# Decode attention on one core: keys and values on two DMA queues with two fixed slots each

## The chip, the cores and the metric

The kernel runs on one core of a Trainium2 chip. The metric is the device time of one execution in microseconds (us). Executions of this kernel are repeatable: the kernel before took 1296.13 to 1296.38 us in four executions. The span of a profile is about 2 us shorter than the time of the same execution. The program uses one core, so there is no comparison of dies to be made.

Words used below: TensorE, VectorE, ScalarE and SyncE are engines of the core, each with its own list of instructions. An engine *issues* a transfer with one instruction; the transfer then stands in that engine's DMA queue (q1 is SyncE's here, q10 ScalarE's) and is carried by the sixteen DMA engines as *packets*, one record of the profile each. It has *landed* when its data can be used. A *slot* is a part of the on-chip buffer `ring` that holds one tile.

## The reference

One decode step of a block: layer norm, attention of one new token over a cache of 8192 positions, output projection, and a gated feed-forward part.

```python
B, Sq, D = 4, 1, 512
H, Sk, Dh = 32, 8192, 128
q = (layernorm(x) @ wq).reshape(B, Sq, H, Dh).transpose(0, 2, 1, 3)
scores = einsum("bhqd,bhkd->bhqk", q, k_cache) * Dh ** -0.5
o = einsum("bhqk,bhkd->bhqd", softmax(scores), v_cache)
h = x + o.transpose(0, 2, 1, 3).reshape(B, Sq, H * Dh) @ wo
hn = layernorm(h)
out = h + (sigmoid(hn @ w_gate) * (hn @ w_up)) @ w_down      # F = 1792
```

All inputs are bfloat16. Each cache has 4 x 32 x 8192 x 128 x 2 bytes = 268 MB, so the caches are 537 MB of the 551 MB that the kernel reads; every byte of them is used once.

## The kernel before

A *tile* is the keys, or the values, of two heads: 128 partitions of 32 KB, 4 MB. There are 64 key tiles and 64 value tiles. The kernel works head by head (`s` counts heads, `t` counts tiles): VectorE transposes the keys of a head into `kT` (four instructions), TensorE multiplies them with the queries (`pe_score`), and after each group of eight heads the exponential is taken. The value product of a head (`pe_pv`) is done ten heads after its scores (`LAG = 10`), so value tile `t` is needed only when key tile `t + 5` has been scored.

All tiles go through four slots of 32 KB per partition, in one order, on one queue: SyncE issues every transfer. A slot is given to the next item in the list, whatever it is.

```python
        items = [("wq", 0)]
        for t in range(NT2 + LAG2):                 # NT2 = 64 tiles, LAG2 = 5
            if t < NT2:
                items.append(("k", t))
            if t >= LAG2:
                items.append(("v", t - LAG2))
            for i in {LAG2 - 4: (0, 1), LAG2 - 3: (2, 3, 4), LAG2 - 2: (5, 6, 7)}.get(t - NT2, ()):
                items.append(("wo", i))             # output weights: eight pieces, among the last values
        items += [("wg", 0), ("wu", 0), ("wd", 0)]  # feed-forward weights: behind everything
        # ... cut: bookkeeping
        for it in items:
            # ... cut: wo goes to kT, wu shares wg's slot
            slot_of[it] = cur
            prev_of[it] = [owner[cur]] if owner[cur] is not None else []
            owner[cur] = it
            cur = (cur + 1) % NS                    # NS = 4
        # ... cut
        for it in items:
            dma_of[it] = [P("sp", fn, (), sem, val) for fn, sem, val in load(it)]
        # ... cut: at the end, an item waits until the slot's former owner is consumed
                op.deps = [sc_of[NST - 1]] if it[0] == "wo" else [consumed[p] for p in prev_of[it]]
```

In the middle of the run keys and values alternate in the list, so a stream already has two slots in effect. At the start the list holds keys 0 to 5 in a row, and they pass through all four slots. The rows of a tile are 32 KB in memory; those of wo and of the down weights are 1 KB, those of the gate and up weights 3584 B.

## Time and profile before

The median is 1296.3 us. What matters of its profile (span 1294.5 us):

| | |
|---|---|
| share of the sixteen DMA engines' time on queue q1 | 99.5% |
| rate in the middle of the span (130 to 1200 us) | 431 GB/s |
| VectorE, TensorE, ScalarE busy | 48%, 39%, 4% of the span |
| last piece of the last value tile is waited for until | 1277.45 us |
| last piece of the down weights is waited for until | 1291.18 us |

The page of the kernel before, the rates in 40 slices of the span, the DMA queues (packets, MB, share of the sixteen engines' time), the chain of work that ended last, and the issues of keys and values (number, size of each, median us from issue to landing):

```profile
GB/s 405 434 428 432 432 428 433 431 430 430 433 431 430 433 429 431 433 427 433 434 426 434 431 427 435 429 431 435 425 434 432 426 435 428 431 434 429 429 376 322
...
q1 hardware_dynamic: 26016, 550.78, 99.5%
...
DMA 81%; PE 12%; SPq 4%; DVE 3%; issue 0%
...
ring<-in_A_k_cache_dram SPq DMA_DIRECT2D x64, 4096.0 KB, 29.7
ring<-in_A_v_cache_dram SPq DMA_DIRECT2D x63, 4096.0 KB, 34.0
```

The engines move 425 to 435 GB/s in every slice but the first and the last two, and the chain that decides the end is 81% DMA. A tile of 4 MB takes 9.71 us at the median between one landing and the next (landing times in the trace), but 30 to 34 us from issue to landing: each waits behind two or three others. So the queue always has work.

The end of the kernel before, from the chain of work that ended last (start us, us, what):

```profile
1279.05 12.10 DMA ring<-in_B_w_down_dram
1291.14 0.04 issue
1291.19 0.60 PE PS L637 x16
...
1291.81 0.20 DVE oT L643
...
1292.37 0.28 DVE o_sb L648
```

The last thing waited for is the last piece of the down weights, and only 1.5 us of compute and the store of the result follow it. The last value piece came 13.7 us earlier (1291.18 - 1277.45); the rest of the attention, the layer norm and the gate and up products ran under the weights' transfer.

There was one short stretch of idle DMA engines in this tail. Value tile 62 takes the slot of value tile 58, which TensorE had finished with at 1221.3 us. But SyncE was in three issues of wo until 1244.6 us and issued the tile only then (start us, us, engine, line, operation), and between 1240 and 1248 us the DMA share was 0.86:

```profile
1221.95 22.66 SPq L220 DMA_DIRECT2D kT<-in_A_wo_dram  x3
1244.66 2.31 SPq L256 DMA_DIRECT2D ring<-in_A_v_cache_dram  x1
...
1240.00:1248.00 8.00, 1.91 (x12) 1.78 (x8) 0.17 (x1) 0.00 (x0) 0.00 (x0) 0.50 0.86 316
```

### The profile page before, as it was taken

Reading aid. Unit: us, or ns where it says so; the run is one execution under the profiler, and the core shown is the slowest. Engines: PE = TensorE matmul, PEld = TensorE weight load, DVE = VectorE, ACT = ScalarE, POOL = GpSimd, SP = SyncE. Lnnn points to the kernel's source line nnn. Section 1 sums busy time; section 2 is a strip of 40 time slices with the busy share of each in tenths; the row PEclk is TensorE's granted clock in tenths of the full one; section 3 lists DMA queues with packets and bytes.
Section 4 is the critical chain, followed back from the end, with each engine's and each line's share of the span. In section 5 each row is a group of like instructions: output and inputs, shape, how many; then the busy total and the mean of one; then the engine's idle time right before and its main releaser. Section 6 shows DMA issues by size and latency. Waiting matters only on the chain.

```text
span 1294.5 us, 12693 instructions
## 1 busy us (share of the span) xinstructions
PE 499.5 (39%) x5827; PEld 193.4 (15%) x5827; DVE 625.4 (48%) x641; ACT 46.1 (4%) x102; POOL 10.6 (1%) x22
## 2 busy tenths in 40 slices
PE   3444334335244244334334334343343343343436
PEld 1011111112011021111111111011110111111114
DVE  5964644535544544535535435445535446445300
ACT  2000000000000000000000000000000000000000
POOL 3000000000000000000000000000000000000000
PEclk9996565665565565565666665665665665656655
DMA  9999999999999999999999999999999999999998
GB/s 405 434 428 432 432 428 433 431 430 430 433 431 430 433 429 431 433 427 433 434 426 434 431 427 435 429 431 435 425 434 432 426 435 428 431 434 429 429 376 322
DMA packets 26076, 551.58 MB, mean 426 GB/s; under 512 B 2340, under 2 KB 8232, under 8 KB 9256
## 3 DMA queue, kind: packets, MB, share of 16 engines
q1 hardware_dynamic: 26016, 550.78, 99.5%
q8 instruction: 45, 0.74, 0.2%
q14 instruction: 7, 0.06, 0.0%
q10 hardware_dynamic: 8, 0.00, 0.0%
HBM read 550.77 MB, written 0.00 MB: 425 GB/s over the span
## 4 chain that ended last, share of the span: by engine, by line
DMA 81%; PE 12%; SPq 4%; DVE 3%; issue 0%
DMA ring<-in_A_v_cache_dram 79%; PE PS L439 7%; PE PS L415 4%; SPq L220 2%; DVE kT L397 2%; SPq L236 1%; DMA ring<-in_A_wq_dram 1%; DMA ring<-in_B_w_down_dram 1%; SPq L228 1%; SPq L256 0%; PE PS L330 0%; DVE Lq L374 0%; DVE ring L347 0%; PE PS L357 0%; PE PS L637 0%
## 5 line engine op out<-in xcount | busy, mean ns | idle before, releaser
L397 DVE STREAM_TRANSPOSE kT<-ring 128x1024 uint32<-128x1024 uint32 x512 | 587.9, 1209 | 578.8 <-DMA ring<-in_A_k_cache_dram 578.6
L415 PE MATMUL PS<-kT,Lq 128*32 128x512 bf16 x2048 | 241.6, 619 | 563.3 <-DVE kT L397 443.8
L439 PE MATMUL PS<-ring,PTz 128*32 128x512 bf16 x2048 | 215.0, 564 | 208.7 <-DMA ring<-in_A_v_cache_dram 208.3
L415 PEld LDWEIGHTS PS<-kT,Lq 128*32 128x32 bf16 x2048 | 69.4, 135 | 692.4 <-DVE kT L397 471.9
L439 PEld LDWEIGHTS PS<-ring,PTz 128*32 128x32 bf16 x2048 | 64.5, 127 | 326.4 <-DMA ring<-in_A_v_cache_dram 197.1
L474 ACT ACTIVATE negm<-PS 128x1 f32<-128x1 f32 x16 | 2.7, 171 | 1156.3 <-PE PS L470 1156.3
L511 DVE TENSOR_SCALAR Zs<-PS,rinv 128x512 f32<-128x512 f32 x16 | 11.6, 723 | 36.4 <-PE PS L439 36.4
L506 ACT ACTIVATE PTz<-PS 64x512 bf16<-64x512 f32 x32 | 18.9, 592 | 16.5 <-PE PS L492 16.1
L518 PE MATMUL PS<-SelZ,Zs 128*128 128x8 f32 x128 | 19.1, 276 | 0.9 <-DVE Zs L511 0.9
L518 PEld LDWEIGHTS PS<-SelZ,Zs 128*128 128x128 f32 x128 | 17.6, 213 | 10.6 <-issue 8.9
L453 DVE TENSOR_REDUCE mx<-PS 128x1 f32<-128x512 f32 x16 | 10.5, 658 | 5.4 <-PE PS L415 5.4
L492 PEld LDWEIGHTS PS<-Sel,E_sb 128*32 128x32 bf16 x1024 | 10.4, 96 | 8.3 <-ACT E_sb L476 7.1
L492 PE MATMUL PS<-Sel,E_sb 128*32 128x32 bf16 x1024 | 11.0, 183 | 1.6 <-ACT E_sb L476 1.1
L476 ACT ACTIVATE E_sb<-PS,negm 128x512 bf16<-128x512 f32 x16 | 11.0, 688 | 0.5
L481 PEld LDWEIGHTS PS<-sig,Gsum 128*128 128x128 f32 x32 | 7.8, 305 | 12.6 <-issue 12.6
L481 PE MATMUL PS<-sig,Gsum 128*128 128x1 f32 x32 | 9.2, 356 | 0.0
L470 PEld LDWEIGHTS PS<-onesf,rowx 1*128 1x128 f32 x32 | 7.3, 281 | 13.0 <-issue 13.0
L470 PE MATMUL PS<-onesf,rowx 1*128 1x1 f32 x32 | 8.6, 336 | 0.0
L523 DVE CAST OT<-PS 128x8 bf16<-128x8 f32 x16 | 2.1, 132 | 11.6 <-PE PS L518 11.6
L347 DVE CAST ring<-PS 128x512 bf16<-128x512 f32 x4 | 2.5, 683 | 10.0 <-PE PS L330 10.0
L485 DVE RECIPROCAL rinv<-PS 128x1 f32<-128x1 f32 x16 | 2.1, 130 | 9.3 <-PE PS L481 9.3
L330 PE MATMUL PS<-ring,xnT 128*32 128x512 bf16 x32 | 3.6, 629 | 6.6 <-DMA ring<-in_A_wq_dram 6.6
(78 smaller groups left out, 81.3 us busy)
## 6 DMA issues: line engine op xcount, KB each, us to landing
ring<-in_A_k_cache_dram SPq DMA_DIRECT2D x64, 4096.0 KB, 29.7
ring<-in_A_v_cache_dram SPq DMA_DIRECT2D x63, 4096.0 KB, 34.0
ring<-in_A_wq_dram SPq DMA_DIRECT2D x1, 4096.0 KB, 12.3
kT<-in_A_wo_dram SPq DMA_DIRECT2D x8, 512.0 KB, 17.3
ring<-in_A_v_cache_dram SPq DMA_DIRECT2D x1, 2048.0 KB, 18.5
ring<-in_A_v_cache_dram SPq DMA_DIRECT2D x2, 1024.0 KB, 18.2
ring<-in_B_w_gate_dram SPq DMA_DIRECT2D x1, 1792.0 KB, 19.9
ring<-in_B_w_up_dram SPq DMA_DIRECT2D x1, 1792.0 KB, 23.5
```

Source lines behind the costliest of these rows:

```text
L220: return [(lambda e: e.dma_start(wo_v[:, HW * t:HW * t + HW, :], A_wo.rearrange("(h p) f -> p h f", p=128)[:, HW * t:HW * t + HW, :]).then ...
L228: return e.dma_start(ringv(slot)[:, c0:c1], kv_src(t, A_v_cache)[:, c0:c1]).then_inc(s_piece[i], 16)
L236: return e.dma_start(wd_v[:, t0:t1, :], B_w_down.rearrange("(t p) f -> p t f", p=128)[:, t0:t1, :]).then_inc(s_piece[3 + i], 16)
L397: return e.transpose(kT[:, buf, i * q:(i + 1) * q].bitcast(U32), ringv(src)[:, base + i * q:base + (i + 1) * q].bitcast(U32))
L415: mm = e.matmul(bS[g % 2][32 * j:32 * (j + 1), :], Lq[:, l0:l0 + 32], rhs, start=(s % GS == 0 and v == 0), stop=(s % GS == GS - 1 and v == 3),
L439: mm = e.matmul(bO[g % 2][32 * rq:32 * (rq + 1), :], PTz[:, g % 2, l0:l0 + 32], ringv(slot)[:, r0 * 128:(r0 + 4) * 128], start=(s % GS == ...
L470: p2_of[g] = P("pe", lambda e: e.matmul(bX[:, 0:1], rowx[0:1, :], onesf[0:1, 0:1], start=True, stop=True), [d2b_of[g], c_ones])
L481: L_of[g] = P("pe", lambda e: e.matmul(bX[:, 0:1], Gsum[:, :], sig[:, 0:1], start=True, stop=True), [exp_of[g], a1_of[g], d_g])
L492: mm = e.matmul(bP[g % 2][32 * a:32 * (a + 1), 32 * rr:32 * rr + 32], E_sb[:, 32 * rr:32 * rr + 32], Sel[:, a, :], start=True, stop=True, ...
L506: return e.activation(dst, src, ACT.Copy)
L511: z_of[g] = P("dve", lambda e: e.tensor_scalar(Zs[:, :], bO[g % 2][:, :], rinv[:, g % 2:g % 2 + 1], None, op0=ALU.mult), [pv_of[g * GS + G ...
L518: mm = e.matmul(bX[:, 256:264], Zs[:, 128 * r:128 * (r + 1)], SelZ[:, r, :], start=(r == 0), stop=(r == 3))
```

## The change

The intent: keys and values each get a queue of their own, keys issued by SyncE and values by ScalarE, so that a value transfer waiting for its slot no longer holds back a key transfer behind it, and the other way round. Each stream gets two fixed slots. The output weights go with the values; the feed-forward weights go on SyncE's queue, once value tile 61 is consumed.

```diff
-        items = [("wq", 0)]
-        # ... cut: the list of items and the rotating slots, as above
+        # ... cut: bookkeeping, and place(), which gives an item a fixed slot
+        place(("wq", 0), 3)
+        for t in range(NT2):
+            place(("k", t), t % 2)
+            place(("v", t), 2 + t % 2)
+        place(("wg", 0), 0)
+        slot_of[("wu", 0)], prev_of[("wu", 0)] = 0, prev_of[("wg", 0)]
+        place(("wd", 0), 1)
 # ... cut
-        for it in items:
-            dma_of[it] = [P("sp", fn, (), sem, val) for fn, sem, val in load(it)]
+        for it in [("wq", 0)] + [("k", t) for t in range(NT2)] + [("wg", 0), ("wu", 0), ("wd", 0)]:
+            issue("sp", it)
 # ... cut
+        issue("act", ("v", 0))
+        issue("act", ("v", 1))
+        wo_after = {NT2 - 3: (0, 1), NT2 - 2: (2, 3, 4), NT2 - 1: (5, 6, 7)}
         for s in range(NST + LAG - 2 + 4):
 # ... cut: the head's work
+            t = (s - LAG - 1) // 2 + 2
+            if (s - LAG) % 2 == 1 and 2 <= t < NT2:
+                for i in wo_after.get(t, ()):
+                    issue("act", ("wo", i))
+                issue("act", ("v", t))
 # ... cut
                 op.deps = [sc_of[NST - 1]] if it[0] == "wo" else [consumed[p] for p in prev_of[it]]
+                if it[0] in ("wg", "wu", "wd"):
+                    op.deps.append(pv_of[NST - 5])
```

No arithmetic and no byte changes. The temporary region for the queries moves from slot 3 to slot 2.

More of the change, by code (lines that the diff above doesn't have):

```diff
@@ L174, in bass_sequential_preLN__mha_block_cached__glu_gated_glu__decode_kernel, with place @@
         HW = H // NWO
-        LAG2 = LAG // 2
-        items = [("wq", 0)]
-        for t in range(NT2 + LAG2):
-            if t < NT2:
-                items.append(("k", t))
-            if t >= LAG2:
-                items.append(("v", t - LAG2))
-            for i in {LAG2 - 4: (0, 1), LAG2 - 3: (2, 3, 4), LAG2 - 2: (5, 6, 7)}.get(t - NT2, ()):
-                items.append(("wo", i))
-        items += [("wg", 0), ("wu", 0), ("wd", 0)]
-        slot_of, prev_of, dma_of = {}, {}, {}
-        owner = [None] * (NS - 1) + [("qr", 0)]
-        uses = [0] * NS
-        cur = 0
-        for it in items:
-            if it[0] == "wo":
-                continue
-            if it[0] == "wu":
-                slot_of[it], prev_of[it] = slot_of[("wg", 0)], prev_of[("wg", 0)]
-                continue
-            slot_of[it] = cur
-            prev_of[it] = [owner[cur]] if owner[cur] is not None else []
-            owner[cur] = it
-            cur = (cur + 1) % NS
+        slot_of, prev_of, dma_of, uses = {}, {}, {}, [0] * NS
+        owner = [None, None, ("qr", 0), None]
+        def place(it, slot):
+            slot_of[it] = slot
+            prev_of[it] = [owner[slot]] if owner[slot] is not None else []
+            owner[slot] = it
+        place(("wq", 0), 3)
[5 more added lines that the diff above has]
+        place(("wd", 0), 1)
         consumed = {}
@@ L256, in load, with issue @@
             return [(lambda e: e.dma_start(dst, src).then_inc(sem, 16), sem, val)]
-        for it in items:
-            dma_of[it] = [P("sp", fn, (), sem, val) for fn, sem, val in load(it)]
+        def issue(eng, it):
+            dma_of[it] = [P(eng, fn, (), sem, val) for fn, sem, val in load(it)]
+        for it in [("wq", 0)] + [("k", t) for t in range(NT2)] + [("wg", 0), ("wu", 0), ("wd", 0)]:
+            issue("sp", it)
         def pool(fn, deps=()):
@@ L334, in bass_sequential_preLN__mha_block_cached__glu_gated_glu__decode_kernel @@
         consumed[("wq", 0)] = p_q[1]
-        QR0 = (NS - 1) * TW
+        QR0 = 2 * TW
         q_ev = []
@@ L356, in pe_qT @@
                     c0 = ((h * 4) + v) * 4
-                    mm = e.matmul(bX[:, c0:c0 + B], ringv(NS - 1)[:, off:off + 128], SelQ[:, j, 0:B], start=True, stop=True)
+                    mm = e.matmul(bX[:, c0:c0 + B], ringv(2)[:, off:off + 128], SelQ[:, j, 0:B], start=True, stop=True)
             return mm
@@ L654, in bass_sequential_preLN__mha_block_cached__glu_gated_glu__decode_kernel @@
         P("sp", sp_out, [o0])
-        for it in items:
-            for op in dma_of[it]:
+        for it, ops in dma_of.items():
+            for op in ops:
                 op.deps = [sc_of[NST - 1]] if it[0] == "wo" else [consumed[p] for p in prev_of[it]]
+                if it[0] in ("wg", "wu", "wd"):
+                    op.deps.append(pv_of[NST - 5])
         prog.resolve(sems)
```

## The prediction

> **What bounds the kernel now.** The transfer of the caches. The page's DMA rows show 551.6 MB at 426 GB/s and 99.5% of the sixteen engines' time on one queue, q1. Successive 4 MB tiles land 9.71 us apart almost without exception (landing times in the trace); each engine carries a tile as eight 32 KB packets of 1.216 us, back to back: 9.73 us, 431 GB/s. The compute engines are far from full: VectorE 48%, TensorE 39%. Per pair of key and value tiles (19.4 us of transfer) VectorE needs 8 x 1.1 = 8.9 us of transposes, TensorE 4 x 1.9 us. The queue's own waits (655 us for the transposes) are slack: a tile lands 30 to 34 us after its issue because it queues behind others.
>
> **What the change moves.** No byte and no arithmetic. An issue costs 0.33 us (timeline), so moving the value issues to ScalarE, busy 46 us in all, saves nothing that was waited for. The Trainium skill, DMA: Bandwidth & Descriptors, section "Issuing engines are not separate DMA queues", says the same: they run on the same 16 engines and interleave. With two queues active each tile should take about 19 us from first packet to landing, the pair 19.4 us as before. In the steady state each queue still has a transfer in flight: a key slot is returned about 9 us after landing, while its neighbour needs 19 us. The middle stays at 430 GB/s.
>
> **Where it should lose a little.**
> 1. Start, +3 us. Value tile 0 is used only after key tile 5 (lag of ten heads), and there are two value slots. From about 66 us (estimate) the key stream runs alone with two slots: transposes of 8.9 us plus about 2.6 us from issue to first packet and completion (first weights: issue to landing 12.33 us, minus 9.73) exceed 9.7 us, about 1 us of idle for each of three tiles.
> 2. Tail, +6 us. Before, the last value piece lands at 1277.4 us of the span, the down weights at 1291.1 us; the chain from the last piece to the end (15.5 us) hides under these 13.7 us. After, the 5.5 MB of weights go on SyncE's queue once value tile 61 is consumed and share the engines with value tiles 62 and 63 and wo. The last value piece should land 0 to 5 us before the last transfer, so 8 to 12 us of chain come into the open; some microseconds of blocked issues in the tail before are regained.
>
> Sum: about +9 us.
>
> **Predicted:** 1305 us; 8 in 10 between 1294 and 1315. Faster by over 2%: 0.01 (idle in the queue is under 1%); within 2%: 0.93; slower by over 2%: 0.06.
>
> **What would show the steps right.** Queues: q1 and a second hardware queue with half of the bytes each, the sum near 99%; middle slices still 425 to 435 GB/s; issue to landing of keys and values 20 to 30 us. Start: between about 80 and 105 us less than 430 GB/s. Tail: last value piece within 5 us of the last weights; the waits of gate and down products for weights gone; the chain of waits ends in some 15 us of compute after the last value piece. ScalarE's wait for value products grows without cost.
>
> **What would make it wrong.** Packets of two queues could each take longer than twice 1.216 us (loss in switching), or overlap better; then the middle moves from 430. If the engines do not share equally (small weight packets against 32 KB), the values may finish earlier and the tail costs nothing. If the streams settle so that one queue runs alone with two slots, bubbles of 1 to 2 us per tile would give over 2%.

## More of the kernel before

Stretches of the span of the kernel before; after the busy times come the granted TensorE clock, the mean busy share of the DMA engines, and GB/s. The three stretches are the time after the start, the middle, and the time just after the last key tile:

```profile
core 0: us, PE busy (x) PEld busy (x) DVE busy (x) ACT busy (x) POOL busy (x), PEclk, DMA share, GB/s
70.00:130.00 60.00, 24.31 (x276) 8.66 (x276) 30.45 (x30) 2.13 (x5) 0.00 (x0) 0.73 1.01 432
130.00:1200.00 1070.00, 408.03 (x4590) 153.02 (x4594) 526.87 (x524) 29.87 (x70) 0.00 (x0) 0.60 1.00 431
1210.00:1242.00 32.00, 17.14 (x205) 7.64 (x205) 7.07 (x11) 3.62 (x7) 0.00 (x0) 0.61 1.00 415
```

The DMA share is 1.00 in all three (it can exceed 1.00 a little, since the packets' records overlap slightly): no time was left to be gained there.

## The result, and the profile after

The changed kernel took 1316.43 us at the median (1314.25 to 1319.87, four executions), the kernel before 1296.3 us. The ratio is 1.0158, with a 95% interval of 1.0134 to 1.0182. Ratios here are the mean time of one kernel's fast runs over that of the other's of the same rounds, so they are not quite the ratio of the medians. The kernel is 20 us slower, outside the predicted range of 1294 to 1315 us, though within the 2% to which the prediction gave 0.93. The profiled execution took 1314.25 us, the fastest of the four, with a span of 1312.3 us, 17.8 us more than before.

The page of the changed kernel, the same rows:

```profile
GB/s 402 432 380 418 434 430 432 430 431 429 430 432 430 431 430 432 431 430 431 429 431 432 431 431 432 431 430 432 428 432 431 430 430 431 431 430 430 356 396 209
...
q1 hardware_dynamic: 12288, 278.14, 49.6%
q10 hardware_dynamic: 13736, 272.64, 48.7%
...
DMA 71%; DVE 24%; ACTq 3%; PE 1%; issue 1%; ACT 0%; DVEq 0%
...
ring<-in_A_k_cache_dram SPq DMA_DIRECT2D x64, 4096.0 KB, 29.6
ring<-in_A_v_cache_dram ACTq DMA_DIRECT2D x63, 4096.0 KB, 32.2
```

Keys and values now share the engines in halves, and the slices from the sixth to the thirty-seventh run at 428 to 432 GB/s as before. What is missing lies in the third and fourth slice (380 and 418) and in the last three (356, 396, 209).

The changed kernel, the same three stretches as before:

```profile
70.00:130.00 60.00, 23.90 (x289) 7.76 (x285) 43.24 (x41) 2.13 (x5) 0.00 (x0) 0.87 0.96 394
130.00:1200.00 1070.00, 388.74 (x4594) 138.97 (x4586) 522.26 (x520) 29.83 (x70) 0.00 (x0) 0.62 1.00 431
1210.00:1242.00 32.00, 9.31 (x170) 3.83 (x165) 11.13 (x13) 2.13 (x5) 0.00 (x0) 0.72 0.83 344
```

The middle is unchanged to the last digit: 1.00 and 431 GB/s. After the start the share is 0.96 over 60 us, after the last key tile 0.83 over 32 us: a few microseconds in each in which engines had nothing to move.

The changed kernel, the end of the chain of work (start us, us, what):

```profile
1274.31 22.60 DMA ring<-in_A_v_cache_dram
...
1296.96 1.07 PE PS L431 x5
...
1298.06 0.76 DVE Zs L503
...
1301.01 1.03 PE PS L578 x32
...
1304.24 0.18 DVE hnT L615
...
1304.47 3.16 PE PS L624 x112
...
1307.99 1.67 PE PS L638 x56
...
1310.24 0.28 DVE o_sb L649
```

The last thing waited for is now the last value piece, at 1296.9 us, and 14 us of compute follow it in the open. To see what makes the 17.8 us, the packets' records of both traces can be summed: the last data packet ends at 1290.65 us before and at 1298.34 us after.

| term (span, us) | before | after | difference |
|---|---|---|---|
| engines idle, 20 to 130 us | 0.0 | 2.7 | +2.7 |
| engines idle, from 1200 us to just before the last packet | 2.1 | 5.0 | +2.9 |
| sum of all packets' times, over sixteen engines | 1290.8 | 1293.6 | +2.8 |
| from the last data packet's end to the end of the span | 3.8 | 14.0 | +10.2 |

Idle is the length of a stretch minus the packets' time in it, summed over pieces of 2 us in which something is missing. The records overlap slightly, so the terms add up to 18.6 and not exactly to 17.8. More than half is compute that used to hide under a transfer. The rest is idle engines at two places, and packets that took longer in sum. The records show where these are: most of the 2.8 us are the first packets after the engines had run empty. They took 1.8 to 1.9 us on average, where a 32 KB packet takes 1.22 us at the median. Between 60 and 120 us they add 2.4 us, and at 1231 us 0.6 us.

So each of the two places costs more than its idle time. The bytes show it directly: the changed kernel has moved its first 27 MB as early as the kernel before (0.1 us later), its first 50 MB 5.1 us later, its first 500 MB 4.9 us later, its first 525 MB 10.7 us later, and all of them 7.7 us later. The start thus costs 5 us, the middle nothing, and the end of the transfers another 2.8 us; with the 10.2 us of compute this is the difference of the spans.

**Where the engines go idle after the start.** Value tiles 0 and 1 fill the values' slots by 66.4 us (landing times in the trace) and cannot be used before key tile 5 is scored. Until then the keys run alone on two slots: a slot comes back only after 9 us of transposes, while the neighbour's transfer takes 9.7 us and was already under way. One such turn: a key slot is free at 81.7 us, the next transfer is issued at 81.75 us and its first packet starts at 82.71 us, 1.0 us later; the neighbour's last packet ends at 81.8 us. The engines start again in this way four times, at 70.6, 82.7, 93.6 and 104.0 us.

**Where they go idle after the last key tile.** Timeline of the changed kernel there (start us, us, engine, line, operation, output and inputs, and in brackets the idle time before it and what ended it). L389 is the transpose, L407 the scores, L431 the value product, L245 the issue:

```profile
1218.43 9.13 DVE L389 STREAM_TRANSPOSE kT<-ring 128x1024 uint32<-128x1024 uint32 x8 [10.21 <-DMA ring<-in_A_k_cache_dram]
...
1227.61 1.11 PE L407 MATMUL PS<-kT,Lq 128*32 128x512 bf16 x16 [0.90 <-DVE kT L389]
...
1228.53 1.05 PE L431 MATMUL PS<-ring,PTz 128*32 128x512 bf16 x16
...
1229.64 0.33 ACTq L245 DMA_DIRECT2D ring<-in_A_v_cache_dram  x1
...
1230.77 1.05 PE L431 MATMUL PS<-ring,PTz 128*32 128x512 bf16 x16 [0.98 <-DMA ring<-in_A_v_cache_dram]
...
1243.53 1.90 PE L431 MATMUL PS<-ring,PTz 128*32 128x512 bf16 x16 [9.35 <-DMA ring<-in_A_v_cache_dram]
```

Key tile 63 is transposed from 1218.4 us on. Value tile 58 has landed at 1221.1 us, but in the program the value product of its second head stands behind the scores of the last head, and these need the last transpose; in the trace it starts right after them (1228.53 after 1227.61). Only then is the slot of value tile 58 free, and value tile 60 is issued at 1229.64. Value tile 59 is practically in by then: the product that waited for it starts at 1230.77. With no keys left and no third value slot the engines run dry. (The stretch from 1240 to 1248 us, which had idle engines before, is full now: a DMA share of 1.06.)

**Why the last value piece comes so late.** The feed-forward weights are issued at 1259.9 us and land while three pieces of wo and value tile 63 are still in ScalarE's queue. DMA queues of the changed kernel from 1269 to 1279 us, with packets, MB and share of the engines' time:

```profile
q1 hardware_dynamic: 859, 3.02, 77.3%
q10 hardware_dynamic: 858, 0.89, 26.5%
```

One queue carries gate and up weights (3584 B packets), the other wo (1 KB packets). The engines take 859 packets from the one and 858 from the other. The order of the records shows turns of one packet, too: where the start of a packet fits the end of just one other (within 6 ns), that other is of the other queue in 176 of 179 cases. So the weights, which nobody needs yet, get 77% of the bytes (3.02 of 3.91 MB), and wo, behind which value tile 63 waits, gets 23%. From 1283 to 1290 us it is the other way round, with value pieces (8 and 16 KB packets) beside the last of wo and the down weights (1 KB):

```profile
q10 hardware_dynamic: 288, 2.65, 91.4%
q1 hardware_dynamic: 286, 0.28, 11.9%
```

### The profile page after: what moved, and what is told of

Same layout as the page of the kernel before. It is cut to its first block, busy times and chain, and to the rows that moved or that the text cites. A ratio compares the mean times of both kernels' runs of the same rounds, so it can differ in the third digit from the quotient of the medians.

```text
span 1312.3 us, 12694 instructions
## 1 busy us (share of the span) xinstructions
PE 473.4 (36%) x5827; PEld 176.8 (13%) x5827; DVE 625.6 (48%) x641; ACT 46.0 (4%) x102; POOL 10.6 (1%) x22
## 4 chain that ended last, share of the span: by engine, by line
DMA 71%; DVE 24%; ACTq 3%; PE 1%; issue 1%; ACT 0%; DVEq 0%
DMA ring<-in_A_k_cache_dram 66%; DVE kT L389 22%; DMA ring<-in_A_v_cache_dram 3%; ACTq L209 2%; DMA ring<-in_A_wq_dram 1%; ACTq L217 1%; DVE mx L445 1%; ACTq L245 0%; PE PS L322 0%; DVE Lq L366 0%; DVE rowx L457 0%; PE PS L624 0%; PE PS L431 0%; DVE mrow L455 0%; DVE ring L339 0%
## 5 line engine op out<-in xcount | busy, mean ns | idle before, releaser
L389 DVE STREAM_TRANSPOSE kT<-ring 128x1024 uint32<-128x1024 uint32 x512 | 588.2, 1209 | 591.1 <-DMA ring<-in_A_k_cache_dram 591.1
L407 PE MATMUL PS<-kT,Lq 128*32 128x512 bf16 x2048 | 217.6, 566 | 773.5 <-DVE kT L389 606.5
L431 PE MATMUL PS<-ring,PTz 128*32 128x512 bf16 x2048 | 210.1, 553 | 33.9 <-DMA ring<-in_A_v_cache_dram 33.6
L407 PEld LDWEIGHTS PS<-kT,Lq 128*32 128x32 bf16 x2048 | 53.9, 119 | 914.8 <-DVE kT L389 673.0
L431 PEld LDWEIGHTS PS<-ring,PTz 128*32 128x32 bf16 x2048 | 64.8, 125 | 132.8 <-issue 81.0
L510 PEld LDWEIGHTS PS<-SelZ,Zs 128*128 128x128 f32 x128 | 16.7, 204 | 10.2 <-issue 8.4
L484 PEld LDWEIGHTS PS<-Sel,E_sb 128*32 128x32 bf16 x1024 | 11.3, 100 | 9.1 <-ACT E_sb L468 6.7
L578 PE MATMUL PS<-OT,kT 128*128 128x4 bf16 (+2 forms) x160 | 4.6, 167 | 11.3 <-DMA kT<-in_A_wo_dram 11.0
L578 PEld LDWEIGHTS PS<-OT,kT 128*128 128x128 bf16 x160 | 4.4, 103 | 12.2 <-issue 11.9
## 6 DMA issues: line engine op xcount, KB each, us to landing
ring<-in_A_k_cache_dram SPq DMA_DIRECT2D x64, 4096.0 KB, 29.6
ring<-in_A_v_cache_dram ACTq DMA_DIRECT2D x63, 4096.0 KB, 32.2
ring<-in_A_v_cache_dram ACTq DMA_DIRECT2D x2, 1024.0 KB, 21.8
ring<-in_B_w_up_dram SPq DMA_DIRECT2D x1, 1792.0 KB, 21.8
```

Of the source, the lines that this page charges most:

```text
L389: return e.transpose(kT[:, buf, i * q:(i + 1) * q].bitcast(U32), ringv(src)[:, base + i * q:base + (i + 1) * q].bitcast(U32))
L407: mm = e.matmul(bS[g % 2][32 * j:32 * (j + 1), :], Lq[:, l0:l0 + 32], rhs, start=(s % GS == 0 and v == 0), stop=(s % GS == GS - 1 and v == 3),
L431: mm = e.matmul(bO[g % 2][32 * rq:32 * (rq + 1), :], PTz[:, g % 2, l0:l0 + 32], ringv(slot)[:, r0 * 128:(r0 + 4) * 128], start=(s % GS == ...
L484: mm = e.matmul(bP[g % 2][32 * a:32 * (a + 1), 32 * rr:32 * rr + 32], E_sb[:, 32 * rr:32 * rr + 32], Sel[:, a, :], start=True, stop=True, ...
L510: mm = e.matmul(bX[:, 256:264], Zs[:, 128 * r:128 * (r + 1)], SelZ[:, r, :], start=(r == 0), stop=(r == 3))
```

## The experiments

Two theories were put against each other. Mine: the queues cost nothing; the loss is made of fixed slots (idle engines at the start and the end) and of weights that overtake value tile 63 by taking turns with wo. The rival: a second queue itself costs time, or slow draining of the values explains the tail and the weights do not matter. The kernel before was run in the same rounds; its medians there were 1296.44 us (first four experiments) and 1296.35 us (last three). "Less than the change" below refers to the first measurement of the changed kernel, 1316.43 us; measured again in the rounds of the last three it took 1315.11 us, so such differences are good to about 1 us. All kernels gave correct results.

### The weights wait until wo has landed

```diff
                 if it[0] in ("wg", "wu", "wd"):
-                    op.deps.append(pv_of[NST - 5])
+                    op.deps.append(dma_of[("wo", NWO - 1)][0])
```

> Only the feed-forward weights' issue is moved: SyncE waits until the last piece of wo has landed, not until value tile 61 is used. Theory (the weights' packets alternate one for one with wo's 1 KB packets and so hold value tile 63 back): value tile 63 lands about 10 us earlier, the compute after the last transfer falls from 12.6 us to about 2 us, time about 1304 to 1308 us. Rival (the tail is long because two value slots drain slowly, the weights do not matter): time stays within 3 us of 1316.

Measured: 1306.09 us (1305.31 to 1307.39), 10.3 us less than the change. Waits of TensorE for wo in the last stretch (engine, line and output, what it waited for: us in total, times, longest us), first the change, then this kernel:

```profile
PE PS L578 <- DMA kT<-in_A_wo_dram: 11.0, 1, 11.0
```

```profile
PE PS L578 <- DMA kT<-in_A_wo_dram: 1.1, 1, 1.1
```

The last value product now starts at 1288.0 us instead of 1297.0, the last data packet (now of the down weights) ends at 1298.7 us, and 4.7 us follow it instead of 14.0 (about 2 us were expected). The transfers end as late as in the change (1298.7 against 1298.3 us): only the order of what lands has changed. The theory predicted 1304 to 1308; the rival, that the weights do not matter, falls.

### Rotating slots, two queues

The edit takes the list of items and the rotation of four slots from the kernel before, keeps keys on SyncE and values on ScalarE, and issues a value tile where the former owner of its slot is consumed. The eight pieces of wo go in one row ahead of value tile 63 (a second difference from the change, not tested by itself), because ScalarE would otherwise stand in their issue when the last exponential is due.

```diff
-        place(("wq", 0), 3)
-        # ... cut: fixed slots
+        # ... cut: items and rotating slots as in the kernel before
-        issue("act", ("v", 0))
-        issue("act", ("v", 1))
-        wo_after = {NT2 - 3: (0, 1), NT2 - 2: (2, 3, 4), NT2 - 1: (5, 6, 7)}
+        act_at = {}
+        for t in range(NT2):
+            kind, o = prev_of[("v", t)][0]
+            act_at.setdefault(2 * o + 1 + (LAG if kind == "v" else 0), []).append(("v", t))
+        last = 2 * (NT2 - 5) + 1 + LAG
+        act_at[last] = [("wo", i) for i in range(NWO)] + act_at[last]
 # ... cut: in the loop over heads
+            for it in act_at.get(s, ()):
+                issue("act", it)
```

> Two queues as in the change, but the four slots rotate over keys and values as before (at the start keys get all four, in the tail values get all four); wo goes in one piece ahead of value tile 63. Theory (fixed slots cost the idle engines, 2.6 us between 70 and 120 us and about 5 us after key tile 63): both idles vanish, time about 6 to 8 us less than the change. Rival (two queues themselves cause the idle): both idles stay, time as the change.

Measured: 1308.63 us (1308.55 to 1308.81), 7.8 us less than the change. The two idle stretches in this kernel:

```profile
70.00:130.00 60.00, 23.15 (x265) 7.77 (x269) 37.69 (x36) 2.13 (x5) 0.00 (x0) 0.56 1.01 433
1210.00:1242.00 32.00, 16.11 (x205) 7.61 (x205) 11.29 (x14) 2.13 (x5) 0.00 (x0) 0.68 1.00 429
```

Both are back at 1.01 and 1.00 with two queues active, so the second queue is not what makes the engines idle; the fixed slots are. The last data packet ends at 1290.8 us as in the kernel before (1290.65), not at 1298.3, and the packets' times sum to 1291.1 us. Its first 50 MB come 0.1 us earlier than in the kernel before. So the fixed slots account for the whole delay of the transfers' end, the longer packet times included. The other loss stays, as it should: the last value piece lands last of all, 15.9 us before the end of the span, and TensorE waits 22.1 us for wo.

### Rotating slots, and the weights wait

Both edits together.

> Both edits together: two queues, rotating slots, weights after wo. Theory (the loss is slots plus weights, the queues are free): time within 3 us of before, 1294 to 1300 us. Rival (two queues cost something in the middle or by themselves): over 1303 us.

Measured: 1297.25 us (1296.97 to 1297.68), a ratio of 1.0007 to before with an interval of 0.9991 to 1.0024. This is 19.2 us less than the change; the single edits gave 10.3 and 7.8. Its three stretches:

```profile
70.00:130.00 60.00, 23.88 (x285) 8.27 (x289) 36.52 (x36) 2.13 (x5) 0.00 (x0) 0.59 1.00 431
130.00:1200.00 1070.00, 408.18 (x4562) 153.35 (x4554) 526.64 (x524) 29.83 (x70) 0.00 (x0) 0.60 1.00 431
1210.00:1242.00 32.00, 15.39 (x205) 6.80 (x205) 11.30 (x14) 2.13 (x5) 0.00 (x0) 0.65 1.00 430
```

Two queues with the slots of before, and with the weights behind wo, take the time of before, within the interval. The rival, over 1303 us, falls: a cost of the second queue above some 3 us, or a gain above 1 us, lies outside the interval.

### Fixed slots, one queue

The slots of the change, but SyncE issues everything in the order of before.

```diff
-        for it in [("wq", 0)] + [("k", t) for t in range(NT2)] + [("wg", 0), ("wu", 0), ("wd", 0)]:
+        # ... cut: the list of items as in the kernel before
+        for it in items:
             issue("sp", it)
 # ... cut: no issues by ScalarE, no wait of the weights for value tile 61
```

> The fixed slots of the change, but all transfers issued by SyncE on one queue in the order of before. Theory: the start is worse than in the change, since keys run alone on two slots from the first tile: about 7 us idle before 90 us; the tail as before, with no weights ahead of value tile 63 and little idle; time about 1301 to 1305 us. Rival (the second queue is the whole loss): time as before, 1296 us.

Measured: 1305.81 us (1305.53 to 1307.6), a ratio of 1.0077 (1.006 to 1.0094) to before. One queue, and still 9.4 us lost, a little more than the 1301 to 1305 us that were expected. Its start, and the time after its last key tile:

```profile
20.00:70.00 50.00, 16.32 (x171) 4.66 (x168) 40.66 (x43) 3.50 (x8) 0.00 (x0) 1.00 0.86 356
1210.00:1242.00 32.00, 12.54 (x177) 4.69 (x165) 11.13 (x13) 2.79 (x6) 0.00 (x0) 0.63 0.91 385
```

The idle of the start is 6.9 us between 20 and 130 us, as expected (with one queue the keys run alone on two slots from the first tile on); with the slow first packets the first 50 MB come 8.7 us later than in the kernel before, nearly the whole loss. In the stretch after the last key tile the expectation missed a little: 2.8 us idle, where I expected hardly any. The rival, that the second queue is the whole loss, falls.

### Small packets for the gate and up weights

This run asks how two queues share the engines. The gate and up weights are fetched in seven column pieces each, so that their rows, and so their packets, are 512 B.

```diff
+            if kind in ("wg", "wu"):
+                NP = 7
+                W = F // NP
+                # ... cut: semaphore value counts the pieces
+                for i in range(NP):
+                    def f(e, c0=i * W, c1=(i + 1) * W):
+                        return e.dma_start(wv[:, :, c0:c1], src.rearrange("(c p) f -> p c f", p=128)[:, :, c0:c1]
+                                           ).then_inc(sem, 16)
```

> The change, with the gate and up weights fetched in seven column pieces each, so that their rows and packets are 512 B and not 3584 B; issued at the same moment as in the change. It tells how the engines share. Theory (one packet of each queue in turn, whatever its size): wo with its 1 KB packets then takes about two thirds of the bytes and not a quarter, lands about 6 us earlier, the last value piece lands about 1288 us instead of 1297 us, though the weights come less efficiently; time 1306 to 1312 us. Rival (the queues share bytes or time equally): the last value piece stays within 2 us of 1297 us and the time within 3 us of the change or above it.

Measured: 1309.72 us (1308.45 to 1311.11), 5.4 us less than the change in the same rounds (1315.11, below). Queues in a stretch of this run with wo on the one and the gate weights on the other (1270 to 1274 us):

```profile
q10 hardware_dynamic: 869, 0.86, 69.8%
q1 hardware_dynamic: 876, 0.43, 40.4%
```

Again nearly as many packets of each queue, 876 and 869; of the bytes wo now has two thirds, 0.86 of 1.29 MB, as expected. The wait of TensorE for wo shrinks from 11.0 to 3.9 us, and the last value product starts at 1289.8 us. Making a transfer less efficient (the packets' times sum to 1298.1 us, 4.5 us more) made the kernel faster, because the transfer that was in the way got fewer bytes per turn. A sharing by bytes or by time would not have moved it.

### The weights behind the values on one queue

```diff
-        for it in [("wq", 0)] + [("k", t) for t in range(NT2)] + [("wg", 0), ("wu", 0), ("wd", 0)]:
+        for it in [("wq", 0)] + [("k", t) for t in range(NT2)]:
             issue("sp", it)
 # ... cut: behind value tile 63 in ScalarE's order
+        for it in [("wg", 0), ("wu", 0), ("wd", 0)]:
+            issue("act", it)
```

> The change, with the gate, up and down weights issued by ScalarE behind value tile 63 on its queue, so the tail is one queue in the order of before; fixed slots stay. Theory: the compute after the last transfer falls to about 2 to 3 us, the idle of the start (2.6 us) and of the tail (5 us) stays; time 1303 to 1308 us, as the run in which the weights waited for wo. Rival (weights on a second queue do not matter): 1313 us or more.

Measured: 1305.89 us (1305.31 to 1306.85). After the last data packet 3.8 us follow, as before. The idle stays, 3.0 us at the start and 6.6 us after the last key tile, a little more than expected. This agrees with the run in which the weights waited for wo: two different ways of keeping the weights out of wo's way give 1306 us.

### The change again

> The changed kernel unaltered, on the chip of these runs, for a comparison in the same rounds and a second trace. All theories: 1314 to 1320 us; idle near 2.6 us between 70 and 120 us and near 5 us between 1220 and 1240 us, the last value piece within 3 us of the last transfer. If its time spreads over some us again, the second trace should show which of these three terms varies.

Measured: 1315.11 us (1314.05 to 1317.03), a ratio of 1.0146 (1.0129 to 1.0163). The second trace has the same make-up: 3.1 us idle at the start, 5.4 us after the last key tile, 14.0 us after the last data packet. The spread between executions was not explained. It goes with the fixed slots (1.5 to 5.6 us between the fastest and the slowest of four, in five kernels with them, against 0.3 and 0.7 us in the two with rotating slots), but the two traces differ by only 0.9 us in span, so they do not show which wait varies.

No version beat the kernel before, and the experiments point to none that would: the best with two queues is level with it, and of the idle time in the kernel before about 2 us lie ahead of the first packet and 2.1 us in the tail, 0.3% together.

## Why the prediction was right or wrong

- **What bounds the kernel, and that the middle stays: right.** 431 GB/s and a DMA share of 1.00 between 130 and 1200 us in both profiles, and two queues with the old slots take 1.0007 of the time before. The Trainium skill, DMA: Bandwidth & Descriptors, section "Issuing engines are not separate DMA queues", says that transfers issued by several engines run on the same 16 DMA engines and interleave. This agrees: 431 GB/s with one queue and with two.
- **The start, +3 us: right in place and cause, too small.** There are 2.7 and 3.1 us of idle in two traces, at the predicted place, and gone when the slots rotate. But the first packet after each of four stretches without work took 1.8 to 1.9 us and not 1.2 us, which the prediction did not count; with these 2.4 us the start costs 5 us.
- **The last value piece within 5 us of the last transfer, and 8 to 12 us of chain in the open: right.** The last value packet ends 2.1 us before the last packet of all; 10.2 us more than before follow after it.
- **The tail as a whole, +6 us: wrong. This is the step that failed.** The prediction set 8 to 12 us of open compute and then took off "some microseconds of blocked issues in the tail before are regained". The open compute came as said (+10.2 us). The blocked issue was regained too: the idle engines between 1240 and 1248 us, 1.6 us by the records, are gone. What the prediction did not have is a new idle of 5.0 us between 1220 and 1232 us, where value tile 60 cannot be issued before the last key tile is scored. There the transfers fall a further 5.8 us behind (4.9 to 10.7 us), and by the end they have made up 3.0 us, so that the net is a loss of 2.8 us where a gain was put. With the 10.2 us of compute the tail costs 13.0 us and not 6. With the 4.9 us of the start this is the difference of the spans, 17.8 us, within rounding.
- **Why the idle was not seen.** The prediction looked for idle at the start, where values wait for keys. It did not follow the same two-slot limit to the end, where the release of value tile 58 waits for the scores of the last key tile. The old list gave the values all four slots there; a stream had two slots in effect only in the middle.
- **How the engines share: half right.** The prediction named unequal sharing as a risk, but expected it to favour the values, whose packets are 32 KB. It did favour those of value tile 62: 2.20 MB against 0.14 MB of the weights from 1261 to 1267 us. It missed that between tile 62 and tile 63 stands wo with 1 KB packets, so that the weights' 3584 B packets got 77% of the bytes there.
- **Issue to landing 20 to 30 us: a little off.** 29.6 us for keys and 32.2 us for values. The median of the timed executions lies 2 us above the profiled one, which the prediction had no means to see.

## What to carry to other kernels

In this kernel, whose DMA engines were busy nearly all the time, a second queue did not make it faster (a ratio of 1.0007), but it removed an order: what was behind something in one queue then ran beside it, in turns of one packet each (859 against 858), so that the transfer with the larger rows took the larger share (77%). Before splitting a queue, list what its order was protecting, above all at the end, where one transfer hides the compute that follows another; keep that order with a wait where it matters. Count a buffer split by stages too: a shared pool of four may be two and two in the middle, and still four for one stream at the start and at the end, when the other stream has nothing to fetch.

## What the Trainium skill lacked or had wrong

- DMA: Bandwidth & Descriptors, section "Queues, rings and completion order", says that an engine goes round its queue rows packet by packet. The runs agree (859 packets against 858, and 876 against 869 of the profile's packets). It lacks the consequence: the bytes are shared as the packets' sizes, 77% to 23% for 3584 B against 1 KB. It also speaks of packets of typically about 9 to 17 descriptors; here the turns are single records of the profile, each one row (176 of 179 that could be matched). How many descriptors a record stands for is not shown.
- The same page, section "Issuing engines are not separate DMA queues", calls the time that an issue takes usually small relative to the transfer. For tiles of 4 MB it was 0.33 us at the median here, but an issue of a 512 KB piece of wo with 1 KB rows lasted up to 11.3 us of the 25.2 us to its landing, with other transfers ahead of it, and held up what its engine was to do next.
- The same page, section "Specifications", gives 512 B as the least transfer for line rate. Here the packets of 512 B took 27 ns at the median (512 / 27 = 19.0 GB/s on an engine; the run with small weight packets), those of 1 KB 47 ns (21.8 GB/s), those of 3584 B 142 ns (25.2 GB/s), those of 32 KB 1216 ns (26.9 GB/s).
- I found no page that says that two streams that share the engines equally need buffers counted by stage. Here two fixed slots a stream left the engines idle for 2.7 us after the start and 5.0 us in the tail, while rotating slots left 0.0 and 1.6 us in the same stretches of the run with two queues.
